# Values by halves of the queries in the full layers of a four-layer attention kernel

## The chip, the cores and the metric

The kernel runs on one core of a Trainium2 chip. The metric is the device time of one launch in microseconds (us); a lower time is better. The engines named below are TensorE (PE; its weight loads are listed apart as PEld), VectorE (DVE), ScalarE (ACT), GpSimd (POOL) and the queue of SyncE (SP), which issues the DMAs.

## The reference

Four layers of multi-head attention are applied in turn to one sequence of S = 2048 tokens with D = 512 features, H = 32 heads of 16 features each. Layers 0 and 2 attend to a sliding window of 256 keys, layers 1 and 3 ("full layers") to all 2048 keys. The input is float32.

```python
def _B_ref(x, wqkv, wo):                      # full; _A_ref is the same with a mask of 256 keys
    B, S, D = x.shape
    H = 32; Dh = D // H
    qkv = (x @ wqkv).reshape(B, S, 3, H, Dh).transpose(2, 0, 3, 1, 4)
    q, k, v = qkv[0], qkv[1], qkv[2]
    scores = jnp.einsum("bhqd,bhkd->bhqk", q, k) * Dh ** -0.5
    p = softmax(scores, axis=-1)
    o = jnp.einsum("bhqk,bhkd->bhqd", p, v)
    return o.transpose(0, 2, 1, 3).reshape(B, S, D) @ wo

x = A_x
x = x + _A_ref(_layernorm(x), A_wqkv, A_wo)
x = x + _B_ref(_layernorm(x), B_wqkv, B_wo)
x = x + _A_ref(_layernorm(x), A_wqkv, A_wo)
x = x + _B_ref(_layernorm(x), B_wqkv, B_wo)
```

## The kernel before

**Places of a full layer.** A full layer runs over 4 blocks `c` of 512 queries and 8 groups `qd` of four heads; layer 3 takes the groups two at a time for all blocks, layer 1 all eight for one block after the other. One (block, group) is called a quad here; a layer has 32. A quad has 16 key tiles `j` of 128 keys, and each tile has two score pairs `pr` (two heads each). `attn_full` (L784) makes the scores of one pair with eight matmuls of 64 rows by 32 columns, which run beside each other in the array (`exps`, L737, L747), into a PSUM tile `s` of which there are two, and ScalarE writes the exponentials of the whole 128 x 1024 tile to an SBUF tile `e` (L752), of which there are EB = 6, used in turn. A stretch of PE's order from one score pair to the next is called a place; the places of a quad are counted n = 2j + pr, from 0 to 31.

**Values.** `pv` (L794) multiplies the exponentials of a key tile, all four heads, by the values: eight float32 matmuls of 512 queries into the two PSUM tiles `acc`. They read both `e` tiles of the tile's two pairs. `pvq` holds those not yet put out. `flush(1)` (`flush`, L755) puts out all but the newest, in the even places behind the scores; at j = 2 it stands behind the second pair. The last values of a quad are followed in the queue by `epilogue` (L704): DVE transposes both `acc` (L712, L715), and only then may the next quad's first values write there.

**Side units.** Projections, values and output products of the layer beside, or of the same one, are cut into units (`project`, `values`, `wo`, `wo_part`). In a full layer a unit of `mms` (L419) consists of groups of eight matmuls (64 x 32 in the array, 512 or 256 columns, L431) that sum into one PSUM tile, `PH["pair"]`, of which there is one. The unit's two row halves are joined by DVE with a copy and an addition (`joined`, L443, L449 and L450), scaled (L540, L541), stored by DMAs of SP and squared by POOL (L546). `squares` (L559) then sums the squares per head on PE (L566), into the same PSUM tile; these sums are put off in `pend` and put out by `settle`, at the latest by the next unit's `mms`.

**What sets PE's order.** PE's order is the order in which the Python program emits its matmuls; the other engines' instructions are ordered by a scheduler with priorities. `attention` (L1000) drives it: a modelled clock, advanced by `spent`, decides when a work may be taken. `Side.step` and `Side.share` (L953, L969) are called once per key tile and take a matmul group from the first ready work as long as a budget allows and the clock has passed `PH["free"]`, which `mms` sets 1.6 or 2.2 past a unit's last group. At the end of a group of two heads' blocks in layer 3 `sd.finish()` emits what is left.

Of the kernel before, what the change touches and what calls it, by code (L numbers as in the profile page):

```python
# [19 lines left out]
P = 128  # L20
# [11 lines left out]
MM = 0.222  # L32
HEAD_START = 100
EB, XB, XNB, WB, VB, OB = 6, 4, 4, 2, 3, 5
L_MIN = 2.0 ** -90
# [151 lines left out]
def fast_path(ctx, tc, flag, a_x, a_wqkv, a_wo, b_wqkv, b_wo, out):  # L187
# [214 lines left out]
    def phase(l):  # L402

        PH["full"], PH["win"] = l is not None and l % 2 == 1, l is not None and l % 2 == 0
        if PH["full"] or not PH["win"] and "pool" not in PH or l is None and PH.get("pair"):
            ps_x.close()
            PH["pool"] = ps_x.enter_context(tc.tile_pool(name=f"ps_x{l}", bufs=1 if PH["full"] else 2, space=bass.MemoryType.PSUM))
            PH["pair"] = PH["pool"].tile([P, 2, QC], F32, name=f"s{l}") if PH["full"] else None

# [9 lines left out]
    def mms(ps, pairs, after=1.6, us=MM):  # L419


        if PH["full"] and pend:
            settle()
            PH["free"] = clock[0] + 1.6
            yield 0.1
        for i, (a, b) in enumerate(pairs):
# [9 lines left out]
            if i < len(pairs) - 1:  # L436
                if PH["full"]:
                    yield us
            else:
                PH["free"] = clock[0] + after  # L440
    TERMS = ((0, 0), (0, 1), (1, 0))
# [117 lines left out]
    def squares(n, sqs):  # L559

        ph = bank(True)
        for t, sq in sqs.items():
            if PH["full"]:
                for r in range(2):
                    half = slice(R * r, R * r + R)
                    nc.tensor.matmul(ph[32 * t:32 * t + 32, r], hsum[half], sq[half], start=True, stop=True, skip_group_check=True)  # L566
            else:
                nc.tensor.matmul(ph[32 * t:32 * t + 32, :], hsum, sq, start=True, stop=True, skip_group_check=True)
        return joined(n, ph, slice(0, P) if len(sqs) > 1 else quarters(*sqs))

# [4 lines left out]
    def keys(l, c, act, ht=None, first=None):  # L575
        sqs = yield from project(l, 1, c, act, ht, first)

        def rest():
# [4 lines left out]
            with tc.high_priority(HEAD_START):  # L583
                nc.vector.tensor_reduce(KM[l][r, c:c + 1], ph[r], axis=AX.X, op=ALU.max)
        pend.append((clock[0] + 3.6, rest))

    def queries(l, c, act, ht=None, first=None):
        sqs = yield from project(l, 0, c, act, ht, first)

        def rest():  # L590
# [3 lines left out]
            if l % 2:  # L594
                r = quarters(ht)
                nc.vector.tensor_scalar(m[r], ph[r], -0.515, None, op0=ALU.mult)
            else:
                kx = vp.tile([P, 1], F32, name=f"kx{l}_{c}", tag="kx")
                nc.vector.tensor_reduce(kx, KM[l][:, max(c - 1, 0):c + 1], axis=AX.X, op=ALU.max)
                nc.vector.tensor_scalar(m, ph, kx, -0.515, op0=ALU.add, op1=ALU.mult)  # L600
            for t in sqs:
# [153 lines left out]
    def flush(n):  # L755
        while len(pvq) > n:
            spent(0.88 if PH["full"] else 1.0)
            for f in pvq.popleft():
                f()
# [24 lines left out]
    def attn_full(l, c, qd, kt, qt, a):  # L784
        for j in range(NT):
            es_ = []
            for pr in range(2):
                if pr and j == 2:
                    PH["side"]()
                elif pr:  # L790
                    flush(1)
                es_.append(exps(f"{l}_{c}_{qd}_{j}_{pr}", kt[j // 8], qt, pr, [(j % 8 * P, 0, QC, 0)]))

            def pv(j=j, es_=es_):  # L794
                for h in range(4):
                    for r in range(2):
                        half = slice(R * r, R * r + R)
                        nc.tensor.matmul(acc[r][32 * h:32 * h + DH + 1, :],  # L798
                                         V[l, qd // 4, j // 8][half, j % 8, 4 * (qd % 4) + h, :],
                                         es_[h // 2][half, h % 2, :], start=(j == 0), stop=(j == NT - 1),  # L800
                                         skip_group_check=True)
            if j == 2:
                flush(1)
            else:
                PH["side"]()
            yield pv
# [98 lines left out]
    class Side:  # L905
# [46 lines left out]

        def step(self):  # L953
            self.k += 1
# [6 lines left out]
            if PH["full"]:  # L961
                return self.share()
            s0, due = self.spent, self.cost * self.k / (self.steps - 2)
# [4 lines left out]

        def share(self):  # L969

            self.budget = min(self.budget + max((self.cost - self.spent) / max(self.steps - 3 - self.k, 1), self.least), 0.75)
            self.lag = max(self.lag - max(0.29, self.least), -0.3)
            while self.q and clock[0] >= PH["free"] and self.budget >= MM / 2 and (self.lag < 0.25 or self.budget > 0.45):
                c = self.one()
                if c is None:
                    break
                self.budget -= abs(c)
                self.lag += abs(c)

# [20 lines left out]
    def attention(l, works):  # L1000
# [5 lines left out]
        for t in range(NHT if l == 3 else 1):  # L1006
            for c in range(NQ):
# [10 lines left out]
                for qd in qds:  # L1018
# [6 lines left out]
                    for f in (attn_win if win else attn_full)(l, c, qd, *ops, a):  # L1025
                        clock[0] = max(clock[0], began + (2.4 if win else 1.8))
                        began = clock[0]
                        pvq.append([f])
                        if win:
                            flush(2)  # L1030
                            sd.step()
                            settle(False)
                    pvq[-1].append(lambda l=l, c=c, qd=qd, a=a: epilogue(l, c, qd, a))
                    ops = nxt
# [205 lines left out]
```

## Time and profile before

| | |
|---|---|
| time, median of 3 runs | 2818.84 us (2815.93 to 2823.44) |
| the profiled execution's own time | 2824.82 us |
| its span, first to last instruction | 2823.1 us |
| granted TensorE clock, mean | 0.991 |
| layer 1, first to last exponential | 505.7 to 1469.7 us of the span |
| layer 3, first to last exponential | 1806.3 to 2804.8 us of the span |

The span is one execution taken by the hardware profiler. A group of instructions is given by its line in the code, its engine, its operation and the tiles it writes and reads. The idle time before a group is that of its engine, with what ended it. In the timeline a row merges instructions of one kind that follow each other, with their number (x8), and a long row can therefore overlap the next. One float32 matmul of the code appears as two records, so that the eight of one value step are x16.

### The profile page before, as it was taken

Reading aid. Unit: us, or ns where it says so; the run is one execution under the profiler, and the core shown is the slowest. Engines: PE = TensorE matmul, PEld = TensorE weight load, DVE = VectorE, ACT = ScalarE, POOL = GpSimd, SP = SyncE. Lnnn points to the kernel's source line nnn. Section 1 sums busy time; section 2 is a strip of 40 time slices with the busy share of each in tenths; the row PEclk is TensorE's granted clock in tenths of the full one; section 3 lists DMA queues with packets and bytes.
Section 4 is the critical chain, followed back from the end, with each engine's and each line's share of the span. In section 5 each row is a group of like instructions: output and inputs, shape, how many; then the busy total and the mean of one; then the engine's idle time right before and its main releaser. Section 6 shows DMA issues by size and latency. Waiting matters only on the chain.

```text
span 2823.1 us, 112536 instructions
## 1 busy us (share of the span) xinstructions
PE 2537.5 (90%) x50557; PEld 1121.1 (40%) x50557; DVE 1247.0 (44%) x2545; ACT 2385.4 (84%) x2687; POOL 592.1 (21%) x1129
## 2 busy tenths in 40 slices
PE   8989999989999999999998899889889898888887
PEld 4333344444434443444443333534444443333332
DVE  7678765122343133223335667333445444344333
ACT  3566664899999999999985766599899999999997
POOL 2477661001101000000015777000000000000000
PEclk9999999999999999999999999999999999999999
DMA  6877775222242223222326554523334333333331
GB/s 220 218 246 221 207 228 184 91 81 86 80 109 85 67 81 108 76 74 81 112 80 193 168 161 132 144 83 97 108 113 119 113 107 100 102 99 105 102 97 55
DMA packets 317708, 348.15 MB, mean 123 GB/s; under 512 B 113056, under 2 KB 233376, under 8 KB 311200
## 3 DMA queue, kind: packets, MB, share of 16 engines
q1 hardware_dynamic: 317216, 340.86, 40.0%
q8 instruction: 397, 6.50, 1.0%
q14 instruction: 95, 0.78, 0.1%
HBM read 228.07 MB, written 96.99 MB: 115 GB/s over the span
## 4 chain that ended last, share of the span: by engine, by line
ACT 47%; PE 27%; issue 11%; DVE 9%; POOL 3%; DMA 2%; SPq 0%; ACTq 0%; POOLq 0%; DVEq 0%
ACT e L752 46%; PE b L434 9%; PE acc L798 5%; PE s L747 4%; PE acc L836 3%; PE s L431 3%; PE bs L434 2%; POOL sq_h L546 1%; POOL e L826 1%; POOL e L829 1%; DVE j_h L450 1%; DVE j_h L449 1%; POOL wr L344 0%; DVE ot L712 0%; DVE ou L715 0%
## 5 line engine op out<-in xcount | busy, mean ns | idle before, releaser
L752 ACT ACTIVATE e<-s 128x1024 f32<-128x1024 f32 (+2 forms) x2432 | 2252.1, 1048 | 150.7 <-PE s L747 141.5
L747 PE MATMUL s<-qt,kt 64*32 64x512 f16 (+3 forms) x17792 | 992.1, 372 | 180.5 <-ACT e L752 140.6
L798 PE MATMUL acc<-e,vt 64*17 64x512 f32 x16384 | 1096.5, 590 | 4.4 <-DVE ot L712 2.7
L747 PEld LDWEIGHTS <-kt 64*32 64x32 f16 (+1 forms) x17792 | 457.3, 90 | 1074.0 <-issue 974.8
L798 PEld LDWEIGHTS acc<-e,vt 64*17 64x17 f32 x16384 | 288.3, 92 | 76.7 <-issue 8.5
L712 DVE STREAM_TRANSPOSE ot<-acc 128x512 f32<-128x512 f32 x128 | 91.3, 713 | 437.1 <-PE acc L798 366.6
L829 POOL TENSOR_SCALAR_AFFINE_SELECT e<-e 128x256 f32<-128x256 f32 x512 | 228.3, 453 | 126.1 <-ACT e L752 125.4
L733 POOL TENSOR_TENSOR oh<-o,oh 128x512 f16<-128x512 f32 x31 | 36.0, 1163 | 884.7 <-DVE oh L732 878.4
L826 POOL TENSOR_SCALAR_AFFINE_SELECT e<-e 128x256 f32<-128x256 f32 x448 | 199.2, 451 | 76.0 <-ACT e L752 73.6
L836 PE MATMUL acc<-e,vt 128*17 128x384 f32 (+2 forms) x2816 | 202.7, 392 | 5.7 <-POOL e L826 3.6
L434 PE MATMUL b<-xc,w 128*128 128x512 f16 x672 | 157.5, 385 | 9.4 <-DVE sp L541 8.0
L546 POOL TENSOR_TENSOR sq_h<-sp_h 128x512 bf16<-128x512 f16 x27 | 41.1, 1521 | 512.9 <-DVE sp_h L540 494.3
L449 DVE COPY j_h<-s 128x512 f32<-128x512 f32 x27 | 18.5, 685 | 278.5 <-PE s L431 256.4
L546 POOL TENSOR_TENSOR sq<-sp 128x512 bf16<-128x512 f16 x28 | 41.9, 1496 | 412.9 <-DVE sp L540 344.7
L449 DVE COPY jo<-s 128x512 f32<-128x512 f32 x72 | 49.8, 691 | 174.3 <-PE s L431 174.3
L431 PE MATMUL s<-xc,w_h 64*32 64x512 f16 x2592 | 113.3, 380 | 7.5 <-DVE jk L450 6.5
L431 PE MATMUL s<-wo,oh 64*32 64x512 f16 x2592 | 106.9, 379 | 10.3 <-DVE jo L450 6.5
L431 PE MATMUL s<-xc,w 64*32 64x512 f16 x2688 | 112.3, 376 | 3.2 <-DVE vt L656 1.7
L538 ACT ACTIVATE sp<-b,es 128x512 f16<-128x512 f32 x56 | 38.4, 687 | 90.2 <-PE b L434 88.1
L434 PEld LDWEIGHTS <-w 128*128 128x128 f16 x720 | 67.6, 99 | 106.4 <-issue 34.5
L655 DVE COPY vt<-s 128x256 f32<-128x256 f32 (+1 forms) x36 | 18.4, 510 | 206.4 <-PE s L431 206.3
L431 PE MATMUL s<-wv,xc 64*32 64x256 f16 (+1 forms) x3456 | 98.5, 305 | 10.3 <-issue 6.4
(186 smaller groups left out, 2056.4 us busy)
## 6 DMA issues: line engine op xcount, KB each, us to landing
kt<-kf SPq DMA_DIRECT2D x128, 512.0 KB
qt<-qs SPq DMA_DIRECT2D x128, 256.0 KB
xd<-x SPq DMA_DIRECT2D x96, 256.0 KB
x<-xd SPq DMA_DIRECT2D x96, 256.0 KB
w<-wd SPq DMA_DIRECT2D x20, 1024.0 KB
kt<-kw SPq DMA_DIRECT2D x64, 256.0 KB
qs<-sp SPq DMA_DIRECT2D x48, 256.0 KB
wo<-wd SPq DMA_DIRECT2D x12, 1024.0 KB
```

The source lines that it names most:

```text
L431: nc.tensor.matmul(ps[g:g + 32, r], a[half, g:g + 32], b[half], start=(i == 0), stop=(i == len(pairs) - 1), skip_group_check=True)
L434: nc.tensor.matmul(ps, a, b, start=(i == 0), stop=(i == len(pairs) - 1))
L449: nc.vector.tensor_copy(j[rows], ps[rows, 0])
L538: nc.scalar.activation(sp[:, 0], ps, AF.Copy, scale=e)
L546: nc.gpsimd.tensor_tensor(sq, sp[:, 0], sp[:, 0], ALU.mult)
L712: nc.vector.transpose(ot.rearrange("p b r -> p (b r)"), a)
L747: nc.tensor.matmul(ps[out_, h, s0:s0 + wd_], kt[R * h:R * h + R, pr, kc + out_.start:kc + out_.stop], qt[R * h:R * h + R, pr, qc:qc + wd_] ...
L752: nc.scalar.activation(e[:, :, w0:w1], ps[:, :, w0:w1], AF.Exp, scale=SCALE)
L798: nc.tensor.matmul(acc[r][32 * h:32 * h + DH + 1, :], V[l, qd // 4, j // 8][half, j % 8, 4 * (qd % 4) + h, :], es_[h // 2][half, h % 2, :] ...
L826: nc.gpsimd.affine_select(v, v, pattern=[[0, 2], [-1, P]], compare_op=ALU.is_gt, fill=0.0, base=0, channel_multiplier=1)
L829: nc.gpsimd.affine_select(v, v, pattern=[[0, 2], [1, P]], compare_op=ALU.is_ge, fill=0.0, base=0, channel_multiplier=-1)
L836: nc.tensor.matmul(a[32 * h:32 * h + DH + 1, q * P:(q + nb) * P], V[l, (4 * c + j) // 4][:, j % 4, 4 * qd + h, :], es_[h // 2][:, h % 2, s ...
```

## The change

The values of a key tile are put out in two steps, one for each half of the 512 queries (`HQ` = 256), so that there are sixteen matmuls of 256 queries in place of eight of 512. `pvq` holds halves, and in the steady state one half stands behind each score pair, in even and odd places alike. How many halves stay behind is set by the place: none is put out in places 3 and 4, two more than usual stay in the queue up to place 11, one more up to place 19, and places 12 and 20 put out two halves each. The number of `e` tiles stays six.

`Side.step` is called in every place with a `room`: at most 0.46 us (by the model) of side groups in one place, more in places 3 and 4, less in 12 and 20. After a unit `PH["free"]` is 1.7 past its last group in full layers in place of 1.6 or 2.2, and after the sums of squares 2.2 in place of 1.6. The sums of squares are no longer joined by DVE: the maximum is taken over both halves at once, and the scaling of queries' sums is done in two DVE operations from PSUM.

```diff
 HEAD_START = 100
+HQ = QC // 2
 EB, XB, XNB, WB, VB, OB = 6, 4, 4, 2, 3, 5
...
             PH["pool"] = ps_x.enter_context(tc.tile_pool(name=f"ps_x{l}", bufs=1 if PH["full"] else 2, space=bass.MemoryType.PSUM))
+            PH["room"] = 0.0
             PH["pair"] = PH["pool"].tile([P, 2, QC], F32, name=f"s{l}") if PH["full"] else None
...
             settle()
-            PH["free"] = clock[0] + 1.6
+            PH["free"] = clock[0] + 2.2
             yield 0.1
...
             else:
-                PH["free"] = clock[0] + after
+                PH["free"] = clock[0] + (1.7 if PH["full"] else after)
     TERMS = ((0, 0), (0, 1), (1, 0))
...
                     half = slice(R * r, R * r + R)
-                    nc.tensor.matmul(ph[32 * t:32 * t + 32, r], hsum[half], sq[half], start=True, stop=True, skip_group_check=True)
+                    nc.tensor.matmul(ph[32 * t:32 * t + 32, r, :], hsum[half], sq[half], start=True, stop=True, skip_group_check=True)
             else:
                 nc.tensor.matmul(ph[32 * t:32 * t + 32, :], hsum, sq, start=True, stop=True, skip_group_check=True)
-        return joined(n, ph, slice(0, P) if len(sqs) > 1 else quarters(*sqs))
+        return ph
...
             with tc.high_priority(HEAD_START):
-                nc.vector.tensor_reduce(KM[l][r, c:c + 1], ph[r], axis=AX.X, op=ALU.max)
+                nc.vector.tensor_reduce(KM[l][r, c:c + 1], ph[r], axis=AX.XY if PH["full"] else AX.X, op=ALU.max)
         pend.append((clock[0] + 3.6, rest))
...
                 r = quarters(ht)
-                nc.vector.tensor_scalar(m[r], ph[r], -0.515, None, op0=ALU.mult)
+                if PH["full"]:
+                    nc.vector.tensor_scalar(m[r], ph[r, 0], -0.515, None, op0=ALU.mult)
+                    nc.vector.scalar_tensor_tensor(m[r], ph[r, 1], -0.515, m[r], op0=ALU.mult, op1=ALU.add)
+                else:
+                    nc.vector.tensor_scalar(m[r], ph[r], -0.515, None, op0=ALU.mult)
             else:
...
                 nc.vector.tensor_reduce(kx, KM[l][:, max(c - 1, 0):c + 1], axis=AX.X, op=ALU.max)
-                nc.vector.tensor_scalar(m, ph, kx, -0.515, op0=ALU.add, op1=ALU.mult)
+                if PH["full"]:
+                    mk = vp.tile([P, QC], F32, name=f"mf{l}_{c}", tag="dn", bufs=2)
+                    nc.vector.tensor_scalar(mk, ph[:, 0], kx, -0.515, op0=ALU.add, op1=ALU.mult)
+                    nc.vector.scalar_tensor_tensor(m, ph[:, 1], -0.515, mk, op0=ALU.mult, op1=ALU.add)
+                else:
+                    nc.vector.tensor_scalar(m, ph, kx, -0.515, op0=ALU.add, op1=ALU.mult)
             for t in sqs:
...
         while len(pvq) > n:
-            spent(0.88 if PH["full"] else 1.0)
+            spent(0.43 if PH["full"] else 1.0)
             for f in pvq.popleft():
...
             for pr in range(2):
-                if pr and j == 2:
-                    PH["side"]()
-                elif pr:
-                    flush(1)
                 es_.append(exps(f"{l}_{c}_{qd}_{j}_{pr}", kt[j // 8], qt, pr, [(j % 8 * P, 0, QC, 0)]))
-            def pv(j=j, es_=es_):
+                n = 2 * j + pr
+                flush(2 - pr + (1 if n == 3 or 12 <= n < 20 else 2 if 4 <= n < 12 else 0))
+                PH["side"](-0.18 if n in (12, 20) else 0.68 if n in (3, 4) else 0.25)
+            def pv(q, j=j, es_=es_):
                 for h in range(4):
...
                         half = slice(R * r, R * r + R)
-                        nc.tensor.matmul(acc[r][32 * h:32 * h + DH + 1, :],
+                        nc.tensor.matmul(acc[r][32 * h:32 * h + DH + 1, HQ * q:HQ * q + HQ],
                                          V[l, qd // 4, j // 8][half, j % 8, 4 * (qd % 4) + h, :],
-                                         es_[h // 2][half, h % 2, :], start=(j == 0), stop=(j == NT - 1),
-                                         skip_group_check=True)
-            if j == 2:
-                flush(1)
-            else:
-                PH["side"]()
+                                         es_[h // 2][half, h % 2, HQ * q:HQ * q + HQ], start=(j == 0 and q == 0),
+                                         stop=(j == NT - 1 and q == 1), skip_group_check=True)
             yield pv
...
-        def step(self):
+        def step(self, room=0.0):
             self.k += 1
...
             if PH["full"]:
-                return self.share()
+                return self.share(room)
             s0, due = self.spent, self.cost * self.k / (self.steps - 2)
...
-        def share(self):
-            self.budget = min(self.budget + max((self.cost - self.spent) / max(self.steps - 3 - self.k, 1), self.least), 0.75)
-            self.lag = max(self.lag - max(0.29, self.least), -0.3)
-            while self.q and clock[0] >= PH["free"] and self.budget >= MM / 2 and (self.lag < 0.25 or self.budget > 0.45):
+        def share(self, room):
+            self.budget = min(self.budget + max((self.cost - self.spent) / max(2 * (self.steps - 3) - self.k, 1), self.least / 2), 0.45)
+            PH["room"] = min(PH["room"] + room, max(room, 0.46))
+            while self.q and clock[0] >= PH["free"] and self.budget >= MM / 2 and PH["room"] > 0.2:
                 c = self.one()
...
                 self.budget -= abs(c)
-                self.lag += abs(c)
+                PH["room"] -= abs(c)
...
                         began = clock[0]
-                        pvq.append([f])
                         if win:
+                            pvq.append([f])
                             flush(2)
...
                             settle(False)
+                        else:
+                            pvq.extend([lambda f=f, q=q: f(q)] for q in range(2))
                     pvq[-1].append(lambda l=l, c=c, qd=qd, a=a: epilogue(l, c, qd, a))
...
                 if l != 1 or c == NQ - 1:
```

## The prediction

> **What bounds the kernel now.** I read the page first: engine shares, the chain that ended last, the costliest groups.
>
> ```profile
> PE 2537.5 (90%) x50557; PEld 1121.1 (40%) x50557; DVE 1247.0 (44%) x2545; ACT 2385.4 (84%) x2687; POOL 592.1 (21%) x1129
> ...
> ACT e L752 46%; PE b L434 9%; PE acc L798 5%; PE s L747 4%; PE acc L836 3%; PE s L431 3%; PE bs L434 2%; POOL sq_h L546 1%; POOL e L826 1%; POOL e L829 1%; DVE j_h L450 1%; DVE j_h L449 1%; POOL wr L344 0%; DVE ot L712 0%; DVE ou L715 0%
> ...
> L752 ACT ACTIVATE e<-s 128x1024 f32<-128x1024 f32 (+2 forms) x2432 | 2252.1, 1048 | 150.7 <-PE s L747 141.5
> ```
>
> PE is the busiest by share, but the chain runs through the exponentials. So I took the two full layers alone (windows of ACT's L752), one stretch in which ACT is never idle (groups by line, 700 to 800 us), and who waits for whom in each full layer.
>
> ```profile
> 505.60:1469.80 964.20, 948.36 (x1024) 1.00 0.27 84
> 1806.20:2804.90 998.70, 952.11 (x1024) 0.99 0.33 100
> ```
> ```profile
> L752 ACT ACTIVATE e<-s 128x1024 f32<-128x1024 f32 x109 | 100.8, 1059 | 0.0
> ```
> ```profile
> PE s L566 <- POOL sq L546: 4.2, 5, 1.3
> PE s L431 <- issue: 3.1, 3, 2.4
> ...
> ACT e L752 <- PE s L747: 14.2, 17, 2.1
> ...
> ACT e L752 <- PE s L747: 44.7, 46, 4.0
> ...
> PE s L566 <- POOL sq_h L546: 17.1, 26, 2.3
> PE s L431 <- DVE jo L450: 6.1, 4, 1.5
> PE s L431 <- issue: 3.3, 2, 1.9
> ```
>
> 109 exponentials in 100 us without idle time make 0.917 us a place. 1024 places are 939 us, and the layers take 964 and 999: 25 and 60 us, 85 in all, are lost to scores that come late. That is the most this change can win. PE is late because, in its fixed order, it sits before a side unit or a sum of squares whose DVE or POOL input isn't there.
>
> **PE's own cost.** The steady order in the timeline:
>
> ```profile
> 851.40 0.41 PE L747 MATMUL s<-qt,kt 64*32 64x512 f16 x8
> 851.62 1.05 PE L798 MATMUL acc<-e,vt 64*17 64x512 f32 x16
> 852.48 0.41 PE L747 MATMUL s<-qt,kt 64*32 64x512 f16 x8
> 852.69 0.63 PE L431 MATMUL s<-xc,w 64*32 64x512 f16 x16
> ```
>
> From start to start a score pair takes 0.215, a key tile's values 0.86, a side group about 0.215. A half should take 0.43: as many columns in all, twice the instructions (8,192 matmuls more in the program). Whether matmuls of 256 columns stream as well is shown by the values' side units:
>
> ```profile
> 522.87 0.74 PE L431 MATMUL s<-wv,xc 64*32 64x256 f16 x40
> 523.42 0.41 PE L747 MATMUL s<-qt,kt 64*32 64x512 f16 x8
> ```
>
> Forty take 0.55 us, 0.11 for eight, half of 0.215, so I price the split itself at nothing. The bounds are 0 and, if every added record cost as much as these whole matmuls, 14 ns, 16 x 0.014 = 0.22 us a key tile. Of that a place gets 0.11: 0.215 + 0.43 + 0.11 + 0.15 of side groups = 0.90, still under 0.917, but it would lengthen the release below by 0.11 (+28 us in all). The side groups are the same 768 and 648 in both built orders. A place now holds 0.215 + 0.43 + 0.15 = 0.79 on the average, where today even places hold 1.07 and odd ones the side.
>
> The Trainium skill (TensorEngine Tiling (Array Packing), section Instruction Overhead) states some 60 cycles of overhead for each matmul on this chip. The row above shows 14 ns for a load and a matmul together, which agrees with it only if the tiles hide most of it; the rule's own result stands among the rivals.
>
> **The wait that is added.** The exponential of place n writes the buffer of place n - 6, and may start only when the second half of that key tile's values has read it. In the built order of before this release always stands places ahead. In the changed one the queue is two halves longer in places 4 to 11, and the exponentials of places 6, 8, 10 and 12 wait for the half that PE issues in the same place, right behind that place's scores: 4 in each of 64 quads, 256 waits, none of them there before. When would they otherwise start? A score pair n starts as soon as the exponential n - 2 frees its PSUM tile. Two narrow windows and a late case:
>
> ```profile
> 851.18 1.09 ACT L752 ACTIVATE e<-s 128x1024 f32<-128x1024 f32 x1
> ...
> 852.10 1.08 ACT L752 ACTIVATE e<-s 128x1024 f32<-128x1024 f32 x1
> ```
> ```profile
> 905.08 0.41 PE L747 MATMUL s<-qt,kt 64*32 64x512 f16 x8
> 905.30 1.05 PE L798 MATMUL acc<-e,vt 64*17 64x512 f32 x16
> 905.62 1.02 ACT L752 ACTIVATE e<-s 128x1024 f32<-128x1024 f32 x1 [0.28 <-PE s L747]
> ```
>
> Scores start at 851.40 and their exponential at 852.10, 0.70 later. The late case shows the least it can be: 0.54, which is 0.215 of streaming and 0.325 from PE's end to ACT. So scores may be 0.16 late at no cost. A release has 0.215 + 0.43 + 0.325 = 0.97, which is 0.27 past 0.70. A delayed exponential lasts 1.02 in place of 1.09, which wins 0.06 back: 0.21 each, and 256 x 0.21 = 54 us. The bounds: if the release had no tail at all, 0.215 + 0.43 = 0.645 lies before 0.70, so 0; if the scores ahead start 0.16 late each time, 0.43, so 110. I take 54, for the tail is that of the nearest row. Queued behind the waiting exponential are ACT's next ones, and the scores of two places on wait for it; with 0.79 of work in a place PE catches up, so nothing else is late.
>
> **The sums of squares.** What they wait for today:
>
> ```profile
> 2084.76 0.41 PE L431 MATMUL s<-xc,w_h 64*32 64x512 f16 x8
> 2085.24 0.69 DVE L449 COPY j_h<-s 128x512 f32<-128x512 f32 x1 [13.64 <-PE s L431]
> 2085.97 0.69 DVE L450 TENSOR_TENSOR j_h<-s,j_h 128x512 f32<-128x512 f32 x1
> 2086.70 0.49 DVE L540 TENSOR_SCALAR sp_h<-j_h,es 128x512 f16<-128x512 f32 x1
> 2087.36 1.52 POOL L546 TENSOR_TENSOR sq_h<-sp_h 128x512 bf16<-128x512 f16 x1 [24.41 <-DVE sp_h L540]
> ...
> 2088.92 0.39 PE L566 MATMUL s<-sq_h,hsum 64*32 64x512 bf16 x2 [0.30 <-POOL sq_h L546]
> ```
>
> The unit's last group starts at 2084.76, its squares are summed at 2088.92: 4.16 through DVE and POOL, and the change leaves this path as it is. Today the order puts most sums four places behind the last group (3.67), so PE is blocked 0.5 and ACT loses nothing. In the changed order "free" is 1.7 and places are counted singly: of 34 sums 20 stand three places behind (2.75 us), 5 at 3.2, 7 at 2.0 to 2.3, and 2 far off. What a blocked PE costs:
>
> ```profile
> 900.84 0.41 PE L566 MATMUL s<-sq,hsum 64*32 64x512 bf16 x6
> 902.54 0.39 PE L566 MATMUL s<-sq,hsum 64*32 64x512 bf16 x2 [1.30 <-POOL sq L546]
> 903.24 2.10 ACT L752 ACTIVATE e<-s 128x1024 f32<-128x1024 f32 x2 [1.06 <-PE s L747]
> ```
>
> PE stood 1.70 and the exponential came 0.70 after the release. Applied to the new place: scores and a half 0.645, blocked 4.16 - 2.75 = 1.41, then 0.70, together 2.76, where the next exponential was due at 0.917 + 0.70 = 1.62. It is 1.14 late, 1.1 after what it wins back. The five at 3.2 stand behind two halves and cost the same, three of the seven stand in places without values and do too; the other four 1.6. That is 28 x 1.1 + 4 x 1.6 = 37 us. Bounds: 8, if each unit ran one place (0.917) ahead of the order's count, and 45, with 1.3 more for six of them that meet the epilogue's transposes. Less DVE work per sum (the join's 0.69 + 0.69 against one longer reduction) lies on a DVE that is 44% busy; it counts only where a unit stands right behind the sums, which is so in three places: some 2 us more each, 6.
>
> **What is left of today's losses.** Four forced ends in layer 3 cost most today:
>
> ```profile
> 1988.87 0.84 PE L431 MATMUL s<-wo,oh 64*32 64x512 f16 x24 [1.54 <-DVE jo L450]
> ...
> 1990.05 2.10 ACT L752 ACTIVATE e<-s 128x1024 f32<-128x1024 f32 x2 [2.15 <-PE s L747]
> ```
>
> In the new order the unit ahead ends 0.64 earlier, so ACT loses about 1.25 and not 2.2: 5 us remain of 9. PE's stalls on "issue", 3.1 and 3.3, depend on nothing edited: 8 with their wake. Place 20 of some twenty quads holds two halves and a side group, 0.215 + 0.86 + 0.215 = 1.29, 0.37 over, 0.16 of it covered: 5. Waits of units for a join's 0.69 + 0.69 fall away mostly, being spaced 2.3 or more. For these and the short losses that no wait shows I keep 10. DMAs of the side units move with them by a place or two on SP's queue; PE waits for none in the rows above, and the loads of scores are issued a quad ahead. If that cover went, one load would stop ACT.
>
> **Sum.** 54 + 37 + 6 + 5 + 8 + 5 + 10 = 125 us of lost time in place of 85: 40 us more. The profiled execution's own time is 2824.82 (span 2823.1), so 2865 by it; it lies 6 us above the median of the runs, 2818.84, and so the forecast is 2859. Its own range, with the release at 0.15 to 0.30 and the sums at 15 to 45, is 2825 to 2890.
>
> **The rivals.** *The release is hidden* (the other side): the half is done before the exponential is due, because PE's end reaches ACT sooner for a buffer than for scores. It decides at 0.70 us from the scores' start. Without its 54: 125 - 54 = 71, 14 less than today, 2805; with the sums at their lower bound too, 42, which is 2776. For it: 0.645 of pure streaming is under 0.70. Against it: the 0.325 tail of the row above. *The sums cost little*, the release stands: 125 - 29 = 96, 2830. For it: places stretch where ACT is late, which gives the squares time. Against: the path of 4.16 is fixed and 20 orders leave 2.75. *Each matmul has a fixed cost*, so that halves are dearer than half: the value records take 0.86 / 16 = 54 ns each today, and if half of that stayed with every record, a half would take 16 x (27 + 13.5) = 0.65 and a place 0.215 + 0.65 + 0.15 = 1.01. That is over 0.917 by 0.095, PE would bound both layers, and 2048 x 0.095 = 195 us come on top: near 3050. The forty in 0.55 speak against it. This is what the page of the Trainium skill named above would make of the change: 60 cycles are 25 ns at 2.4 GHz, by an estimate from that page.
>
> **Chances.** Forecast 0.66; sums cost little 0.14, of which 0.02 lie near no change; release hidden 0.16, of which 0.06 lie there, for it brings sums between its two figures; fixed cost 0.04. About 0.3%, 8.5 us, is what a measurement of this kernel can tell. Slower: 0.66 + 0.12 + 0.04 = 0.82. Same: 0.02 + 0.06 = 0.08. Faster: 0.10. The range 2810 to 2900 leaves out most of the hidden release and the fixed cost, and the ends of the forecast.
>
> **What would show it.** ACT's exponentials waiting for PE's acc (the halves) 256 times, by 0.1 us of idle time each (0.27 less the 0.17 by which records overlap, 852.27 against 852.10), some 26 us, in places 6, 8, 10 and 12 alone. PE's waits for POOL's squares rising from 21 to about 40 us. Halves 0.43 apart from start to start. Layer 1 near 982 and layer 3 near 1021 us. It is wrong if those exponentials show no such releaser, if halves take over 0.5, or if the two layers together come under 1963.

## The result and the profile after

| | before | after |
|---|---|---|
| time, median of 4 runs each, same chip | 2820.36 us (2815.93 to 2823.44) | 2901.74 us (2898.56 to 2907.06) |
| ratio | | 1.0292, 95% interval 1.0268 to 1.0315 |
| the profiled execution's own time | 2824.82 us | 2904.52 us |
| layer 1, first to last exponential | 964.0 us | 1006.5 us |
| layer 3, first to last exponential | 998.5 us | 1039.9 us |

The kernel became slower by 81 us, where 40 were forecast (2859 against 2902). The page of the changed kernel: the engines' shares, the chain of waits by line, the exponentials and the values, and the queue that carries PE's instructions (packets, MB, share).

```profile
PE 2615.5 (90%) x66941; PEld 1361.8 (47%) x66941; DVE 1223.0 (42%) x2496; ACT 2403.3 (83%) x2687; POOL 588.6 (20%) x1129
...
ACT e L763 39%; PE acc L808 9%; PE b L436 9%; PE s L758 8%; PE acc L842 3%; PE s L433 3%; PE bs L436 1%; POOL sq_h L548 1%; POOL wr L345 1%; POOL e L832 1%; POOL e L835 1%; DVE xh L483 0%; DVE xh L477 0%; DVE xn L477 0%; PE s L568 0%
...
L763 ACT ACTIVATE e<-s 128x1024 f32<-128x1024 f32 (+2 forms) x2432 | 2269.8, 1047 | 215.7 <-PE s L758 155.5
L808 PE MATMUL acc<-e,vt 64*17 64x256 f32 x32768 | 1326.1, 378 | 24.4 <-issue 18.2
...
q8 instruction: 525, 8.60, 1.2%
```

The exponentials are now 39% of the chain where they were 46%, and their idle time is 215.7 us where it was 150.7. PE has 66,941 matmul records where it had 50,557, and its instructions come in 525 packets of 16 KB in place of 397: the 128 more are the 8,192 added matmuls, 256 bytes each. The two full layers in the windows of ACT's L763 (length, busy time, granted clock, DMA share, GB/s):

```profile
505.35:1511.86 1006.51, 958.41 (x1024) 1.00 0.26 81
1844.44:2884.39 1039.95, 959.77 (x1024) 0.99 0.32 97
```

Against 939 us each, 67 and 101 us are lost, 168 in all where the prediction had 125 and before has 85. The clock and the DMA share stayed (before: 1.00 and 0.99, 0.27 and 0.33). Who waits in layer 1 and then in layer 3 (waits for PE's inputs; total, times, longest):

```profile
PE acc L808 <- issue: 9.3, 15, 1.4
PE s L568 <- POOL sq L548: 5.8, 6, 1.5
PE s L758 <- issue: 5.2, 7, 1.7
...
PE s L433 <- issue: 0.7, 2, 0.4
...
PE s L568 <- POOL sq_h L548: 32.2, 26, 2.6
PE acc L808 <- issue: 8.9, 10, 2.4
PE s L433 <- issue: 5.6, 4, 2.2
PE s L433 <- DVE jo L452: 4.6, 7, 0.9
PE s L433 <- DVE km L586: 4.5, 4, 1.3
PE s L758 <- issue: 2.7, 5, 0.9
```

PE's waits for the squares are 38 us, as predicted (about 40). What was not predicted is "issue", time in which PE waits for nothing that the profile shows: 32.4 us by these rows (15.2 and 17.2). The same view of before, over the whole span, has 8.6:

```profile
PE s L431 <- issue: 6.4, 5, 2.4
...
PE acc L798 <- issue: 1.7, 2, 1.1
...
PE s L747 <- issue: 0.5, 1, 0.5
```

I split the 168 us by cause: each exponential that ends more than 0.917 us after the one before it is put down to PE's longest wait in the 3.2 us ahead of it, waits for ACT itself left out. In the table, "wake" is the time that ACT loses behind a stall of PE, and "forced ends" are units that the end of a block puts out at once.

| term of the prediction | predicted, us | measured, us |
|---|---|---|
| release waits, places 6, 8, 10, 12 | 54 | 50 (256 of 0.195) |
| sums of squares | 37 | 35 |
| units right behind the sums (DVE's km) | 6 | 12 |
| forced ends (DVE's jo) | 5 | 8 |
| PE's stalls on issue, with their wake | 8 | **42** |
| double halves, the epilogue's transposes, rest | 15 | 21 |
| sum | 125 | 168 |

By the same split before loses 11 us behind stalls on issue.

A release place in the timeline (start, length, engine; places 6 and 7 of a quad of layer 1; the last row is a narrow window on ACT):

```profile
796.64 0.41 PE L758 MATMUL s<-qt,kt 64*32 64x512 f16 x8
796.85 0.63 PE L808 MATMUL acc<-e,vt 64*17 64x256 f32 x16
...
797.77 0.63 PE L808 MATMUL acc<-e,vt 64*17 64x256 f32 x16
798.20 0.41 PE L433 MATMUL s<-wo,oh 64*32 64x512 f16 x8
```
```profile
797.59 1.94 ACT L763 ACTIVATE e<-s 128x1024 f32<-128x1024 f32 x2
```

Place 6's scores start at 796.64, its half ends some 0.43 after 796.85 (the same step to the next group is seen at 797.77 to 798.20), and its exponential starts at 797.59: 0.95 after the scores, where the sum said 0.97.

A stall on issue in place 20 of a quad of layer 1, ahead of its two halves (timeline, loads left out), and the stretches around it (length, then busy time of PE, its loads, DVE, ACT and POOL, granted clock, DMA share, GB/s):

```profile
1151.37 0.41 PE L758 MATMUL s<-qt,kt 64*32 64x512 f16 x8
...
1153.13 1.09 PE L808 MATMUL acc<-e,vt 64*17 64x256 f32 x32 [1.35 <-issue]
...
1153.99 0.44 PE L758 MATMUL s<-qt,kt 64*32 64x512 f16 x8
...
1154.54 1.94 ACT L763 ACTIVATE e<-s 128x1024 f32<-128x1024 f32 x2 [1.39 <-PE s L758]
```
```profile
1148.00:1150.00 2.00, 2.00 (x86) 1.11 (x78) 0.00 (x0) 2.00 (x3) 0.00 (x0) 1.00 0.62 216
1150.00:1152.00 2.00, 1.78 (x64) 0.82 (x49) 0.42 (x1) 2.00 (x3) 0.00 (x0) 1.00 0.15 54
```

The exponentials that these halves read are done, the exponential of place 21 comes at 1154.54, and DVE and POOL have no part in it; PE stands 1.35 us and ACT loses 1.39. In the records of the instruction packets one starts at 1144.84 and the next only at 1150.95 to 1151.93, 6.1 us later, 1.2 us before PE goes on; the windows show a burst of other transfers (share 0.62, 216 GB/s) at 1148 to 1150. All 41 stalls over 0.2 us look so: PE resumes 1.2 to 1.6 us behind the end of a packet. The median distance of packets is 4.0 us in the full layers, and 5.6 in before.

### The profile page after: what moved, and what is told of

Its sections match the earlier page's. It is cut to its first block, busy times and chain, and to the rows that moved or that the text cites. A ratio compares the mean times of both kernels' runs of the same rounds, so it can differ in the third digit from the quotient of the medians.

```text
span 2902.8 us, 145250 instructions
## 1 busy us (share of the span) xinstructions
PE 2615.5 (90%) x66941; PEld 1361.8 (47%) x66941; DVE 1223.0 (42%) x2496; ACT 2403.3 (83%) x2687; POOL 588.6 (20%) x1129
## 3 DMA queue, kind: packets, MB, share of 16 engines
q1 hardware_dynamic: 317216, 340.86, 38.4%
## 4 chain that ended last, share of the span: by engine, by line
ACT 40%; PE 35%; issue 11%; DVE 7%; POOL 4%; DMA 2%; SPq 0%; ACTq 0%; POOLq 0%; DVEq 0%
ACT e L763 39%; PE acc L808 9%; PE b L436 9%; PE s L758 8%; PE acc L842 3%; PE s L433 3%; PE bs L436 1%; POOL sq_h L548 1%; POOL wr L345 1%; POOL e L832 1%; POOL e L835 1%; DVE xh L483 0%; DVE xh L477 0%; DVE xn L477 0%; PE s L568 0%
## 5 line engine op out<-in xcount | busy, mean ns | idle before, releaser
L763 ACT ACTIVATE e<-s 128x1024 f32<-128x1024 f32 (+2 forms) x2432 | 2269.8, 1047 | 215.7 <-PE s L758 155.5
L808 PE MATMUL acc<-e,vt 64*17 64x256 f32 x32768 | 1326.1, 378 | 24.4 <-issue 18.2
L758 PE MATMUL s<-qt,kt 64*32 64x512 f16 (+3 forms) x17792 | 1032.5, 376 | 161.4 <-ACT e L763 103.5
L808 PEld LDWEIGHTS acc<-e,vt 64*17 64x17 f32 x32768 | 606.1, 93 | 188.8 <-issue 38.4
L433 PE MATMUL s<-xc,w_h 64*32 64x512 f16 x2592 | 138.8, 381 | 4.5 <-DVE km L586 4.5
L433 PE MATMUL s<-xc,w 64*32 64x512 f16 x2688 | 140.7, 378 | 1.3 <-DVE j L452 1.3
L433 PE MATMUL s<-wv,xc 64*32 64x256 f16 (+1 forms) x3456 | 134.7, 306 | 6.5 <-issue 6.3
L433 PE MATMUL s<-wo,oh 64*32 64x512 f16 x2592 | 135.0, 378 | 4.6 <-DVE jo L452 4.6
L451 DVE COPY j<-s 128x512 f32<-128x512 f32 x28 | 19.3, 689 | 258.2 <-PE s L433 258.2
L436 PEld LDWEIGHTS <-w 128*128 128x128 f16 x720 | 67.2, 98 | 105.1 <-issue 32.4
```

The lines of the kernel that those rows point to most:

```text
L433: nc.tensor.matmul(ps[g:g + 32, r], a[half, g:g + 32], b[half], start=(i == 0), stop=(i == len(pairs) - 1), skip_group_check=True)
L436: nc.tensor.matmul(ps, a, b, start=(i == 0), stop=(i == len(pairs) - 1))
L451: nc.vector.tensor_copy(j[rows], ps[rows, 0])
L758: nc.tensor.matmul(ps[out_, h, s0:s0 + wd_], kt[R * h:R * h + R, pr, kc + out_.start:kc + out_.stop], qt[R * h:R * h + R, pr, qc:qc + wd_] ...
L763: nc.scalar.activation(e[:, :, w0:w1], ps[:, :, w0:w1], AF.Exp, scale=SCALE)
L808: nc.tensor.matmul(acc[r][32 * h:32 * h + DH + 1, HQ * q:HQ * q + HQ], V[l, qd // 4, j // 8][half, j % 8, 4 * (qd % 4) + h, :], es_[h // 2 ...
```

## The experiments

My theory: doubling the value matmuls costs nothing in streaming, but PE needs a third more instructions in nearly the same time, so that a packet of them that comes late stops it; the releases and the sums cost what was predicted. Rivals: the new order makes the stalls (bursts of two halves), or every matmul has a fixed cost. Each kernel is compared with before on one chip, with an interval.

**The split alone, in the order of before.**

```diff
             def pv(j=j, es_=es_):
-                for h in range(4):
+                for q, h in ((q, h) for q in range(2) for h in range(4)):
...
-                                         es_[h // 2][half, h % 2, :], start=(j == 0), stop=(j == NT - 1),
-                                         skip_group_check=True)
+                                         es_[h // 2][half, h % 2, HQ * q:HQ * q + HQ], start=(j == 0 and q == 0),
+                                         stop=(j == NT - 1 and q == 1), skip_group_check=True)
```

> The order of before, except that a key tile's values are sixteen matmuls of 256 queries, back to back, in the place where eight of 512 stood. No release, sum or unit moves. My theory of the stalls on issue in the changed kernel (some 32 us of PE's idle time where before has 8.6) is that PE waits for its own instructions, of which there are a third more: then they rise here too, to 25 us or more, the queue that carries the instructions moves 525 packets as in the changed kernel, and the time is 20 to 35 us over before, 2840 to 2855. Rival, the new order makes the stalls (two halves in one place, or a side unit behind them): stalls stay near 9 us and the time within 6 us of before. Second rival, each matmul has a fixed cost: a key tile's sixteen take clearly more than 0.86 us from start to start, and the time is above 2900.

Measured: 2875.11 us against 2819.16, ratio 1.0193 (1.0173 to 1.0214). PE's steps and its waits on issue:

```profile
850.55 1.06 PE L799 MATMUL acc<-e,vt 64*17 64x256 f32 x32
851.41 0.41 PE L748 MATMUL s<-qt,kt 64*32 64x512 f16 x8
```
```profile
PE acc L799 <- issue: 21.7, 21, 3.1
...
PE s L432 <- issue: 9.3, 12, 1.6
PE s L748 <- issue: 8.2, 7, 2.4
```

From 850.55 to 851.41 a key tile in halves takes 0.86, as a whole one does: no fixed cost shows, and that rival falls. But the stalls rise from 8.6 to 39.2 us, and by the split by cause 54 us of lost time stand behind them (before: 11). The time rises by 56, more than the 20 to 35 expected, because a stall of PE costs ACT its wake as well: 43 us of the rise stand behind stalls. The new order is not needed for it. The Trainium skill (TensorEngine Tiling (Array Packing), section Instruction Overhead) would have put a cost on each matmul; in eight tiles side by side none is seen here.

**As many instructions more, but in the scores.**

```diff
         for kc, qc, wd_, s0 in pieces:
+            zd = QC // 2 if PH["full"] else wd_
+            for z in range(0, wd_, zd):
...
-                    nc.tensor.matmul(ps[out_, h, s0:s0 + wd_], kt[R * h:R * h + R, pr, kc + out_.start:kc + out_.stop],
-                                     qt[R * h:R * h + R, pr, qc:qc + wd_], start=True, stop=True,
+                        nc.tensor.matmul(ps[out_, h, s0 + z:s0 + z + zd], kt[R * h:R * h + R, pr, kc + out_.start:kc + out_.stop],
+                                         qt[R * h:R * h + R, pr, qc + z:qc + z + zd], start=True, stop=True,
```

> Before, with the scores (not the values) split by halves of the queries: sixteen matmuls of 256 columns for a pair in place of eight of 512, first half first, then the second. That is 16 more records a place in both full layers, 2 MB more of instructions or 128 packets, as many as the split of the values adds. Theory of the instructions: whatever matmuls carry them, stalls on issue rise to 30 to 40 us and the time by 45 to 60, to about 2870, as in the run that split the values alone (2875). Rival, it is something of the float32 values by halves: then stalls stay near 9 us and the time within 10 us of before.

Measured: 2887.00 against 2820.78, ratio 1.0244 (1.0224 to 1.0265); 525 packets.

```profile
PE s L749 <- issue: 21.0, 27, 2.3
...
PE s L431 <- issue: 9.7, 13, 1.9
PE acc L800 <- issue: 8.4, 11, 2.1
```

39.1 us of stalls, and 60 us of lost time behind them, while sixteen matmuls of 256 columns take the same 0.21 us to the next step as eight of 512: it is the number of instructions, whichever matmul carries them.

**The release alone undone.**

```diff
-                flush(2 - pr + (1 if n == 3 or 12 <= n < 20 else 2 if 4 <= n < 12 else 0))
-                PH["side"](-0.18 if n in (12, 20) else 0.68 if n in (3, 4) else 0.25)
+                flush(2 - pr + (1 if n == 3 or 5 <= n < 20 else 2 if n == 4 else 0))
+                PH["side"](-0.18 if n in (5, 20) else 0.68 if n in (3, 4) else 0.25)
```

> The changed kernel, but two halves stand in place 5 (and one in place 12), so that the queue is one half shorter in places 5 to 11 and no exponential's buffer is released in its own place. Theory of the release (256 waits of 0.195 = 50 us): the exponentials waiting for PE's acc vanish, and the time falls by 45 to 52 us, to about 2853. Rival, places 6 to 12 are late through something else that the wait covers (packed places, instructions): the waits vanish, but waits for the scores take their place and the time falls by less than 20. What speaks against a full gain: two halves in place 5 meet the epilogue's transposes of the quad before.

Measured: 2879.10 against 2819.16, ratio 1.0214 (1.0189 to 1.0240): 23 us less than after, not 45. Places 8, 10 and 12 lose nothing regularly any more; place 6 loses 0.16 in most quads, behind the two halves and a side group of place 5, some 7 us. And the stalls on issue rise:

```profile
PE acc L808 <- issue: 23.7, 24, 2.3
PE s L758 <- issue: 10.5, 15, 2.0
PE s L433 <- issue: 6.2, 8, 2.1
```

40.4 us, and the lost time behind them goes from 42 to 56. So of the 50 won some 7 stayed at place 6 and 14 were given back as stalls (168 lost us became 140). These are readings of one trace each, and the runs of this kernel spread over 13 us; why the stalls rose is not shown.

**The sums alone put later.**

```diff
         pend.append((clock[0] + 3.6, rest))
+        if PH["full"]:
+            PH["free"] = clock[0] + 1.5
```

(at both places that put sums off, for keys and for queries)

> The changed kernel, but a unit whose squares are to be summed sets the earliest time of the next emission 1.5 us later, so that the sums stand 4.6 to 5.5 us behind the unit's last group where most stood 2.75. Theory of the sums (35 us of lost time by 34 sums, 1.1 each): PE's wait for POOL's squares falls from 38 us to under 5, and the time by 25 to 32 us, to about 2874. Rival, the sums only meet a loss that another step would show anyway (the queue of instructions, or a unit that then has to come closer to the next): the wait goes, but the time falls by less than 10.

Measured: 2887.29 against 2819.16, ratio 1.0236 (1.0216 to 1.0257), 14 us less than after. PE's wait for the squares:

```profile
PE s L568 <- POOL sq L548: 3.6, 2, 2.2
```

34 of the 38 us of waits went, as expected, but half of the gain came back at once: the units come later, and PE's wait for the joins of the units forced out at a block's end rose.

```profile
PE s L433 <- DVE jo L452: 20.1, 13, 1.9
```

The stalls on issue are 26.7 us here, the least of the kernels with 525 packets and all their loads: they do not grow whenever another wait goes.

**Both edits.**

> Both edits together: the early second half in place 5 and the sums 1.5 us later. If the two losses are separate and add up, 50 + 28 us go and the time is about 2825 (2815 to 2835), still not under before, because the stalls on issue (32 us of idle time, 42 of lost time) stay. If they hide behind each other the time stays over 2845; if the stalls on issue came from those waits too (PE resumes in a burst after each), they fall below 20 us here and the time falls under 2812.

Measured: 2847.91 against 2819.16, ratio 1.0095 (1.0065 to 1.0124), 54 less than after and 23 over the expectation. By the sign set ahead of the run (over 2845) the losses hide behind each other, and the gains do not add: 23 and 14 apart, 54 together. 109 us are lost in the two layers; the squares have under 1 of them and place 6 some 11, but 67 stand behind stalls on issue (49.9 us of idle time, the most of any run). Both waits are nearly gone, and the third loss grew from 42 to 67; what made it grow was not tried apart.

**The same order with whole values.**

(the last kernel, with the eight matmuls of a key tile in the step of its second half)

```diff
-                for h in range(4):
+                for h in range(4 if q else 0):
...
-                        nc.tensor.matmul(acc[r][32 * h:32 * h + DH + 1, HQ * q:HQ * q + HQ],
+                        nc.tensor.matmul(acc[r][32 * h:32 * h + DH + 1, :],
...
-                                         es_[h // 2][half, h % 2, HQ * q:HQ * q + HQ], start=(j == 0 and q == 0),
-                                         stop=(j == NT - 1 and q == 1), skip_group_check=True)
+                                         es_[h // 2][half, h % 2, :], start=(j == 0), stop=(j == NT - 1),
+                                         skip_group_check=True)
```

> The order of the last run (early second half in place 5, sums 1.5 us later), but each key tile's values are again eight matmuls of 512 queries, in the step of its second half; the step of the first half is empty. In the last run 109 us of the exponentials' time were lost, 67 of them behind PE's stalls on issue. Theory of the instructions: with 397 packets in place of 525 these stalls fall back to about 9 us and the loss to some 50, so the time is 2790 (2780 to 2805), under before. Rival, the stalls belong to the new order: they stay over 40 us, and the time stays within 10 us of the last run's 2848 or rises, since whole values make every second place 1.07 long.

Measured: 2849.12 against 2820.78, ratio 1.0107 (1.0083 to 1.0131). The stalls are 3.0 us, and only 4 us of lost time stand behind them, so they belonged to the instructions here too. But the time did not move, for the places became uneven:

```profile
850.34 0.41 PE L762 MATMUL s<-qt,kt 64*32 64x512 f16 x8
850.56 1.05 PE L812 MATMUL acc<-e,vt 64*17 64x512 f32 x16
851.42 0.41 PE L433 MATMUL s<-xc,w 64*32 64x512 f16 x8
851.63 0.41 PE L762 MATMUL s<-qt,kt 64*32 64x512 f16 x8
...
852.44 0.41 PE L762 MATMUL s<-qt,kt 64*32 64x512 f16 x8 [0.39 <-ACT e L767]
```

The place from 850.34 holds scores, a whole key tile and a side group, 1.29 us; the next waits 0.39 for ACT. Some 76 of 111 lost us are such places, with no wait of PE ahead of them. The halves do even out the places, and here that is worth about what their instructions cost. My "2790" left this out.

**Fewer other transfers, the split alone.**

```diff
+    kept = {}
     def load_full(l, c, qd):
+        if l in kept:
+            return kept[l]
...
+        kept[l] = kts, qt
         return kts, qt
```

The kernel leaves out the loads of keys and queries of all quads of a layer but the first, whose data the others then use. The DMA queues of the data move 259.59 MB in place of 340.86; PE's instructions and their order stay.

> As the run that only split the values (2875 us, 39 us of stalls on issue), but the full layers load their keys and queries once a layer and not once a quad: some 1.25 MB less to move in each of 62 quads; 62 quads compute on the keys and queries of the first. What it tells: the instruction packets that end a stall come 5 to 7 us behind the one before them, where 4 is usual, and the DMA engines were busy 0.47 of the 5 us ahead of them, against 0.28 on the average. If the packets are late because other transfers hold the DMA engines, the stalls fall to under 25 us and the time by 15 or more. If PE simply takes its instructions too fast for their queue, whatever else moves, they stay at 35 to 42 and the time falls by less than 6.

Measured: 2840.85 against 2819.97, ratio 1.0081 (1.0054 to 1.0108): 34 us less than with the loads.

```profile
PE acc L804 <- issue: 7.3, 12, 1.3
...
PE s L432 <- issue: 5.9, 8, 1.7
...
PE s L748 <- issue: 2.7, 8, 0.6
```

The same instructions in the same order stall PE 15.9 us in place of 39.2, and the lost time behind the stalls goes from 54 to 26. So the packets are late where other transfers are under way. Before with kept loads was not run; it has 11 us behind its stalls, and could win no more than that this way.

**The same edit in the changed kernel.**

> The changed kernel, but the full layers load their keys and queries once a layer (62 quads compute on the keys and queries of the first); PE's order is not touched. In the changed kernel I put 42 us of the exponentials' lost time down to the stalls on issue, by what stood ahead of each late exponential. If that holds, the same edit that took the other split kernel from 39 us of stalls to 16 and its time down by 34 takes these from 32 to under 16, and the time falls by 20 to 30, to about 2877; the 256 release waits and PE's waits for squares (38 us) stay as they are. If much of those 42 us belongs to the order and only passes behind a stall, the stalls fall and the time by less than 12.

Measured: 2869.91 against 2820.98, ratio 1.0186 (1.0157 to 1.0214), 32 us less than after; the squares' waits stay (38.0 us).

```profile
PE s L568 <- POOL sq_h L548: 32.4, 26, 2.6
...
PE acc L813 <- issue: 4.5, 9, 1.0
...
PE s L758 <- issue: 2.1, 5, 0.5
```

The lost time behind stalls goes from 42 to 12 us, which is the 32 to within 2. So the failed term is shown in the kernel itself, by an edit that touches neither its instructions nor their order.

**Fewer instructions by larger tiles.**

```diff
-            for g in range(0, P, 32 if PH["full"] else P):
+            for g in range(0, P, 64 if PH["full"] else P):
...
-                    out_ = slice(g, g + 32) if PH["full"] else slice(0, P)
+                    out_ = slice(g, g + 64) if PH["full"] else slice(0, P)
```

> Before, with a pair's scores in four matmuls of 64 rows by 64 columns in place of eight of 64 by 32: 1 MB fewer instructions, 64 packets less. Theory of the instructions: before's own stalls on issue, 8.6 us, go to about 2, and the time falls by 5 to 10 if nothing else changes. Rival, changing the tile's shape between scores and values costs time at each change: a pair takes more than 0.215 us from its start to the next matmul, and with 0.1 us per change in 2048 places the time rises by more than 50.

Measured: 3043.65 against 2820.78, ratio 1.0796 (1.0774 to 1.0817).

```profile
899.71 0.41 PE L747 MATMUL s<-qt,kt 64*64 64x512 f16 x4
900.05 1.08 PE L798 MATMUL acc<-e,vt 64*17 64x512 f32 x16
901.06 0.41 PE L747 MATMUL s<-qt,kt 64*64 64x512 f16 x4
```

Scores now take 0.34 to the next step in place of 0.215, and values 1.01 in place of 0.86: a change of the tile's shape costs 0.13 to 0.15 us each time. That it is the change, and not the new shape, shows in the side units, which kept 64x32: a group takes 0.216 to the next group and 0.340 to the next scores. There are 333 packets, but a place with values is 1.35 long, so instructions cannot be saved this way here.

**Before with the sums later, then with the budget spread earlier.** The first has the edit of the sums above; the second adds:

```diff
-            self.budget = min(self.budget + max((self.cost - self.spent) / max(self.steps - 3 - self.k, 1), self.least), 0.75)
+            self.budget = min(self.budget + max((self.cost - self.spent) / max(self.steps - 7 - self.k, 1), self.least), 0.75)
```

> Before, with the sums of squares 1.5 us later (5.3 to 5.5 us behind the unit's last group where most stood 3.67). PE's waits for POOL's squares are 21 us in before and the exponentials lose some 15 behind them. Theory of the sums: the waits fall under 5 us and the time by 10 to 15, to about 2807. Rival, as in the changed kernel, where the same edit brought 14 of the 28 expected: units come late to the forced ends, and PE's waits for the joins rise by as much: 2815 to 2825.

> Before with the sums 1.5 us later (2804), where 30 us of lost time stand behind the join of a unit that the end of a block forced out (1.3 to 1.9 us of side groups in the last place of six blocks of layer 3); here the budget is spread over four steps fewer, so that forced groups are 0.65 to 1.3 us. Expected: half of the 30 goes, 2790 (2785 to 2798). Rival, the units that now stand closer meet joins and sums elsewhere: no change.

Measured: 2803.76 against 2820.78, ratio 0.9942 (0.9925 to 0.9958), and 2793.07 against 2819.97, ratio 0.9914 (0.9889 to 0.9939). In the second the waits for joins, which had grown in the first, are:

```profile
PE s L431 <- DVE jk L450: 7.4, 3, 3.0
PE s L431 <- DVE jo L450: 7.3, 9, 1.9
```

54 us are lost in the full layers in place of 85. This kernel is faster than before, by 0.9%, and than the changed one.

**That kernel with the sums not joined, one part of the change.**

> The last run and one part of the change: the sums of squares are not joined by DVE, the maximum runs over both halves and the scaling of the queries' sums takes two operations from PSUM. Where a unit stands right behind the sums it waits for the read of the shared tile: two operations of 0.69 each in before, one longer one here. Expected 1 to 4 us less than the last run (waits for jk and jq of some 6 us go, waits for km of 1 to 2 us each come). Rival, the longer reduction holds the tile as long: no change.

Measured: 2794.89 against 2819.97, ratio 0.9905 (0.9886 to 0.9924): no change against the last. The waits for jk (7.4 us) became waits for km (5.9).

## Why the prediction was wrong

- **The failed step** is the term "PE's stalls on 'issue', 3.1 and 3.3, depend on nothing edited: 8 with their wake". They depend on how many instructions PE is given, and the change adds 8,192 matmuls. It measured 42 us (11 in before): 34 of the 43 that the sum of lost time was short. The two rows were also only part of before's 8.6 us. The run with the split alone, the one with the scores split and the one with kept loads show it. I had counted the added records and priced their streaming only.
- **The split's streaming**, priced at nothing, was right (0.86 a key tile in both forms). The rival of a fixed cost for each matmul falls, though its sign, dearer because there are more of them, was that of the miss; the price came from fetching, not from executing.
- **The release waits** were right in place and number and nearly in size (0.195 for 0.21). Their idle time is 0.087 us each; the views put most of it down to the exponential ahead, since records overlap, and name PE's acc 36 times, where I had said 256.
- **The sums** were right: 35 for 37, PE's waits for squares 38 for about 40. That they are not made by the loads or the stalls is shown by the run with kept loads; what their removal is worth is less (14 us in the changed kernel, 17 in before), since the forced ends grow.
- **Small terms**: the other 9 of the 43 are units behind the sums 6, forced ends 3 and the rest 6, less the 6 by which releases and sums were too high. In the rest some 9 us are three quads whose first values wait for the epilogue's transposes, which I had not priced. These were read from the trace alone and not tried apart.
- **The sum** added terms as if separate. The runs show that they are not: taking nearly all of the 50 us of release waits away brought 23. The sign was right; with the 34 added, the profiled sum of 2865 becomes 2899, and 2904.52 was measured. The two layers missed their lengths (982 and 1021) by 24 and 19 for the same reasons. The low end of the sum's own range comes to 2821 by its terms, not 2825; nothing hangs on it.

## What to carry to other kernels

Splitting a matmul can cost nothing in streaming, as here, and still add instructions (a third more here) which have to reach PE: count bytes of instructions per us beside columns, and look at the waits on issue and at the queue that carries instructions before an edit that adds matmuls. Losses that PE takes in turn can hide each other, so price an edit by the one that shows next. Where a sum waits for a fixed path through other engines (4.16 us here), spacing by that path paid (17 us in before), but check what it pushes to the block's end.

## What the runs showed of the hardware

- PE's instructions come in 16 KB packets, each of 64 float32 matmuls here, and are late where other transfers run: in the 5 us ahead of a packet that ends a stall the DMA engines are busy 0.47 of the time, ahead of all packets 0.27 (changed kernel). Some stalls come without such a load. In the first 110 us of layer 1, where the values' side units of 256 columns run and a packet comes each 3.7 us (3.9 in the rest of the layer), the changed kernel has 7.6 of its 31.9 us in stalls over 0.2; with kept loads 4.3 us stay there, of 7.0 in all, with the DMA engines busy 0.13 ahead of their packets. Whether it is the DMA engines or the memory that holds a packet up was not told apart.
- The Trainium skill (Runtime: NRT & Kernel Launch, section Instruction fetch mechanics) calls the cost of crossing a 16 KiB block mostly hidden, since the sequencer dispatches slower than blocks arrive. With a packet each 5.6 us that agrees (8.6 us of stalls in before); with one each 4.0 us and all loads under way it doesn't (27 to 50 us; 7 and 16 with the loads kept), and the measurement decides.
- A change of the tile's shape between 64x64 and 64x32 costs PE 0.13 to 0.15 us (1.35 for 1.075 in a place with values).
- A seventh tile `e`, which might also undo the release, was not tried.
